# Sigmoid attention and SwiGLU on one core: an immediate bias for the scores' sigmoids, and the first gates and vals in four parts

## The chip, the core and the metric

The kernel runs on one core of a Trainium2 chip. The metric is the device time of one execution in microseconds (us). A core has a matrix engine (TensorE, "PE" in the profile; its weight loads are listed apart as "PEld"), a vector engine (DVE), a scalar engine that evaluates functions such as the sigmoid (ACT), a general one (GpSimd, "POOL"), and a sync engine that starts transfers here (SP). Each engine runs its own queue of instructions in order, and they wait for one another through semaphores. Matmuls write into PSUM, which has eight banks; each bank holds a 128 x 512 tile of 32-bit numbers.

## The reference

For 8 batches and 12 heads, 448 positions and 64 features per head:

```python
scores = q @ k.T / sqrt(64) - log(448)
attn = sigmoid(scores)                  # no softmax
x = (attn @ v), heads side by side      # 3584 x 768
g = x @ w_gate                          # 768 -> 1536
val = x @ w_val
out = (g * sigmoid(g) * val) @ w_out    # 1536 -> 768
```

The bias of the sigmoid, -log(448), is one number for the whole kernel.

## The kernel before

The attention is cut into 24 units (three for each batch, four heads each). A unit's q and k are loaded, cast to 16 bits into `src`, and transposed into `qkT`: by TensorE for the first six units (line 382), by DMA afterwards (line 408). Its scores are made in seven *bursts* (line 425) of four 64x64 matmuls each, into two banks; each burst is followed by two sigmoids on ScalarE (`sig`, line 446), which read the banks and write the tile `pt`. When enough `pt` tiles are there, the PV matmuls (line 466) multiply them with v, and two casts give two feature chunks `xT` of 128 features each. So a batch has six feature chunks, j = 0 to 5, and unit 0 gives j = 0 and 1, unit 1 gives 2 and 3, unit 2 gives 4 and 5.

The sigmoid takes its bias from a tile of one column, `sbiast`, that is filled once at the start (line 226).

The feed-forward part works through a batch in twelve tiles of 128 hidden features, two at a time (`f1`). For a pair, `joint` makes the gates (`ps_g`) and later the vals (`ps_v`): 48 matmuls each, in *quarters*, that is, in 64x64 pieces of the array (line 517). The upper 64 rows of the array write to the bank of one tile of the pair while the lower 64 rows write to the bank of the other; then the two change places. So a gate has two halves (t = 0 and 1) of 24 matmuls over all six chunks j. Between the halves stands a *turn* (line 502): a no-op on ScalarE that waits for the last matmuls of the first half and for which the first matmuls of the second half wait. ScalarE then makes the sigmoid of the gates (`s`, line 542; no bias), VectorE multiplies it with the gate (`t`, line 548) and with the vals (`hT`, line 555). The output product (`ps_o`) and its sums come later and are not touched.

Weights of gate and val come in four chunks of 384 hidden features: chunk 0 serves the tiles 0 to 2, chunk 1 the tiles 3 to 5, and so on. Each is loaded in three pieces (j in pairs) and cast by GpSimd (line 340). `ORDER` fixes the order of the loads on SP's queue: units 2 and 3 before chunk 0, unit 4 before chunk 1, unit 5 before chunk 2, unit 6 before chunk 3.

The order of the instructions on each engine is not written by hand. Every piece of work is an `op` with an engine, a planned duration, what it depends on, and the banks or buffers that it takes and gives. A dependency can have a lead: the op may begin so long before the other ends. `list_schedule` plays the program with these durations, always taking the first ready op in the order of writing within a window (40 for TensorE, 30 for ScalarE), and what comes out is the order in which the instructions are issued. The planned duration of a sigmoid of the scores is 0.445 us. Once issued, the order on an engine is fixed, and real times follow from the semaphores.

Of the kernel before, what the change touches and what calls it, by code (L numbers as in the profile page):

```python
# [13 lines left out]
SIGM = mybir.ActivationFunctionType.Sigmoid  # L14
# [41 lines left out]
STICK = 0.2  # L56
NEAR = 12
SPREAD = 3
SLOW = 1.0
LATE = 0.1  # L60
FIRST = ()
# [121 lines left out]
def kernel(  # L183
# [10 lines left out]
    nc = tc.nc  # L194

    B, H, S, D = q.shape
# [57 lines left out]
    def op(*a, **kw):  # L254
        o = Op(*a, **kw)
        ops.append(o)
        return o
# [73 lines left out]
    def load_w(w, dst, c, j2, nm):  # L331
        def fl():
            T[nm, c, j2] = staging()[:, 0:2 * CW].rearrange("p (j f) -> p j f", j=2)
            nc.sync.dma_start(
                out=T[nm, c, j2],
                in_=w[j2 * 256:(j2 + 1) * 256, c * CW:(c + 1) * CW].rearrange(
                    "(j p) f -> p j f", p=128))

        def fc():
            nc.gpsimd.tensor_copy(out=dst[c][:, 2 * j2:2 * j2 + 2, :], in_=T[nm, c, j2])  # L340
        uses[0] += 1
        ld = op("SP", 0.6, fl, take=["st"], desc=(256, CW * 4))
        R.setdefault(("w", nm, c), []).append((fc, ld))

    def load_wc(c):
        for w, dst, nm in ((moe_w_gate, wg16, "wg"), (moe_w_val, wv16, "wv")):
            for j2 in range(KC // 2):
                load_w(w, dst, c, j2, nm)

    def cast_wc(c):  # L350
        for nm in ("wg", "wv"):
# [89 lines left out]
    def sig(key, dep, slot):  # L441
        def fn(a):
            def go():
                if a == 0:
                    T[("pt",) + key] = sb.tile([128, 2, S], FP16, tag="pt", bufs=slots["pt"], name="pt")
                nc.scalar.activation(out=T[("pt",) + key][:, a], in_=T[("sc",) + key][a][:, 0:S], func=SIGM, bias=sb_t,  # L446
                                     scale=qkscale)
            return go
        x = op("ACT", 0.445, fn(0), deps=[dep], take=["pt"], give=slot[1:2])
        R["pt ring", key] = x.take  # L450
        R["sig"] = R[("pt",) + key] = op("ACT", 0.445, fn(1), deps=[x and (x, LAT["ACT"] + LATE)], give=slot[:1] + slot[2:])

    def pv(i):

# [40 lines left out]
    def after_ins(x, y):  # L495
        tc.add_manual_dep(x, y.name, mybir.DependencyInfo(mybir.DependencyClass.Sync, mybir.DependencyReason.DATA))

    def turn(a, n):

        def fn():  # L500
            e = {"DVE": nc.vector, "ACT": nc.scalar, "POOL": nc.gpsimd}[TURN]
            T["turn", n()] = e.nop().ins
            for x in T["half", n()]:
                after_ins(T["turn", n()], x)
        return op(TURN, 0.07, fn, deps=[a])

    def quarters(steps, t, n):

        for k, two in enumerate(steps):
            for row in range(2):
                o, w, x = two[row ^ t]
                rs = slice(64 * row, 64 * row + 64)
                for col in range(2):
                    cs = slice(64 * col, 64 * col + 64)
                    mm = nc.tensor.matmul(out=o[cs], lhsT=w[rs, cs], rhs=x[rs], start=t == 0 and k == 0,  # L517
                                          stop=t == 1 and k == len(steps) - 1)
                    if t == 0 and k == len(steps) - 1:
                        T.setdefault(("half", n), []).append(mm.ins)  # L520
                    if t == 1 and k == 0:
                        after_ins(mm.ins, T["turn", n])

    def f1(b, f):

        two = (f, f + 1)
        m, o = divmod(b, 2)

        def both(w, nm, t):
            def fn():  # L530
                if t == 0:
                    T["pair", nm, b, f] = T["pairs"] = T.get("pairs", 0) + 1
                    for n, x in enumerate(two):
                        T[nm, b, x] = bank("ps_" + nm, n)[:, 0:S]
                quarters([[(T[nm, b, x], w[x // FC][:, j, (x % FC) * 128:(x % FC + 1) * 128], T["xT", b, j]) for x in two]
                          for j in range(KC)], t, T["pair", nm, b, f])
            return fn

        def fs(f):
            def fn():  # L540
                t = T["s16", b, f] = sb.tile([128, S], FP16, tag="s16", bufs=slots["s16"], name="s16")
                nc.scalar.activation(out=t, in_=T["g", b, f], func=SIGM)  # L542
            return fn

        def ft(f):
            def fn():
                t = T["t1", b, f] = sb.tile([128, S], FP16, tag="t1", bufs=slots["t1"], name="t1")
                nc.vector.tensor_tensor(out=t, in0=T["g", b, f], in1=T["s16", b, f], op=MULT)  # L548
            return fn

        def fh(f):
            def fn():
                if o == 0 and f == 0:
                    T["hT", m] = sb.tile([128, NF, 2 * S], FP16, tag="hT", bufs=2, name=f"hT_{m}")
                nc.vector.scalar_tensor_tensor(  # L555
                    out=T["hT", m][:, f, o * S:(o + 1) * S], in0=T["v", b, f], scalar=HSC,
                    in1=T["t1", b, f], op0=MULT, op1=MULT)
            return fn
        xs = [(R["xT", b, j], 0.19 * j) for j in range(KC)]
        old = R["f2", m - 2] if m >= 2 and b % 2 == 0 else []  # L560

        def joint(w, nm, deps):
            a = None
            ws = [(x, 0.38 * n) for c in {x // FC for x in two} for n, x in enumerate(R["w16", "w" + nm, c])]
            for t in range(2):
                a = op("PE", 0.19 * KC, both(w, nm, t), mode=("Q", "Q"), take=[] if t else ["P", "P"],
                       deps=xs + deps + ws + [a and turn(a, lambda: T["pair", nm, b, f])])
                banks = banks if t else a.take
            return a, banks
        g, gbank = joint(wg16, "g", [])  # L570
        ts = []
        for n, x in enumerate(two):
            s = op("ACT", 0.45, fs(x), deps=[g], take=["s16"])
            s.first = 2
            ts.append(op("DVE", 0.54, ft(x), deps=[s], take=["t1"], give=s.take + gbank[n:n + 1]))

        def val():
            v, vbank = joint(wv16, "v", old + [(g, 1.0)])
            if f == NF - 2:
                v.give += [x for o, _ in xs for x in o.take]  # L580
            for n, (x, t) in enumerate(zip(two, ts)):
                R["hT", b, x] = op("DVE", 0.54, fh(x), deps=[v, t] + old, give=vbank[n:n + 1] + t.take)
        return val
# [164 lines left out]
    def f2_pair(x, y):  # L748

        two = (x, y)  # L750

        def make(final):
            for f, n in two:
                if n == 1:
                    f["start"](final)

            def fn(t):
                def go():
                    key = two[0][0]["key"] + two[0][1:]
                    if t == 0:  # L760
                        T["pair", key] = T["pairs"] = T.get("pairs", 0) + 1
                        for q, (f, n) in enumerate(two):
                            T[("p",) + f["key"] + (n,)] = bank("ps_o", q)[:, 0:HW]
                    quarters([[(T[("p",) + f["key"] + (n,)], f["spec"][n][0]()[:, x // 2, x % 2], f["spec"][n][1](x))
                              for f, n in two] for x in range(NH)], t, T["pair", key])
                return go
            a = None
            for t in range(2):
                a = op("PE", 0.1625 * NH, fn(t), mode=("Q", "Q"), take=[] if t else ["P", "P"],
                       deps=[d for f, n in two for d in f["spec"][n][2]()] + ([turn(a, lambda: T["pair", two[0][0]["key"] + two[0][1:]])] if t else [(x, LAT["PE"] + LATE) for x in [R.get("turn")] if x]))  # L770
                banks = banks if t else a.take
            R["turn"] = a
            for q, (f, n) in enumerate(two):
                f["P"][n] = a
                f["taken"][n] = banks[q:q + 1]
            for f, n in two:
                f["after"](n, final)
        return make
# [39 lines left out]
    for what in ORDER:  # L818
        if what[0] in "qv":
            loads(int(what.lstrip("qkv")), {"q": "qkv", "qk": "qk", "v": "v"}[what.rstrip("0123456789")])  # L820
        else:
            load_wc(int(what[1:]))
    casts(1)
    NPE = 6

# [138 lines left out]
```

## Time and profile before

| | |
|---|---|
| time, median of 3 | 412.19 us (412.06 to 412.19) |
| span in the profile | 410.0 us, TensorE clock 1.000 |
| TensorE busy | 401.5 us (98%) |
| ScalarE busy | 251.4 us (61%), of it 192.3 in 336 sigmoids of the scores |
| VectorE / GpSimd busy | 229.2 us (56%) / 131.3 us (32%) |
| read from HBM / written | 47.19 MB / 11.01 MB |

The page divides the span into 40 slices of 10.25 us and gives the busy share of each engine in tenths. In a group of instructions, the line names line of code, engine, operation, output<-inputs, shapes and count; behind the first bar are the total busy time and the mean of one in ns, behind the second the idle time of the engine ahead of such instructions and what ended it. Rows of stages give start and end of the stretch, its length, and for each engine the busy time with the number of instructions, then the clock, the DMA share and GB/s. Rows of the chain of waits give start, duration and what the chain went through.

### The profile page before, as it was taken

The numbers are of one execution on the slowest core, as the hardware profiler recorded it, in microseconds if no ns is written. First come the engines' busy times: TensorE is split into PE (matmuls) and PEld (weight loads), VectorE is DVE, ScalarE is ACT, GpSimd is POOL, SyncE is SP. The second block draws the span as 40 slices with busy tenths as digits, with TensorE's granted clock in tenths as the row PEclk, the third lists the DMA queues.
The fourth block names the chain that finished last, engine by engine and source line by source line (L and its number), as shares of the span: only waits on it lengthen the run. The fifth ranks groups of instructions, "written<-read, shape, count | busy, mean of one in ns | idle before, by whom it ended". The sixth has DMA issues, their size and how long they took to land.

```text
span 410.0 us, 17536 instructions
## 1 busy us (share of the span) xinstructions
PE 401.5 (98%) x7872; PEld 305.8 (75%) x7872; DVE 229.2 (56%) x420; ACT 251.4 (61%) x472; POOL 131.3 (32%) x194
## 2 busy tenths in 40 slices
PE   8989999999999999999999999999999999999995
PEld 3435666689977787666889877778999989997663
DVE  3424544457685457564555564645465655556874
ACT  5997789877878844378748567576576662111100
POOL 1888866556442312522322313422310200000000
PEclk9999999999999999999999999999999999999999
DMA  7999999999665518454864654663500302010335
GB/s 267 380 376 376 375 309 309 272 317 261 184 182 146 151 70 189 151 96 136 209 182 89 175 116 148 180 128 135 122 5 3 80 2 65 19 42 15 103 83 148
DMA packets 64794, 67.57 MB, mean 165 GB/s; under 512 B 35536, under 2 KB 60880, under 8 KB 64720
## 3 DMA queue, kind: packets, MB, share of 16 engines
q1 hardware_dynamic: 62864, 59.78, 51.6%
q0 software_dynamic: 1536, 6.29, 5.9%
q8 instruction: 61, 1.00, 1.0%
q10 hardware_dynamic: 320, 0.39, 0.3%
q14 instruction: 13, 0.11, 0.1%
HBM read 47.19 MB, written 11.01 MB: 142 GB/s over the span
## 4 chain that ended last, share of the span: by engine, by line
PE 90%; ACT 7%; issue 1%; DMA 1%; DVE 0%
PE ps_v L517 26%; PE ps_g L517 26%; PE ps_o L517 16%; PE ps_o L669 7%; PE ps_sc L425 7%; PE ps_pv L466 7%; ACT pt L446 6%; DMA st<-in_q_dram 1%; PE ps_tr L382 1%; ACT s L542 0%; PE ps_warm L810 0%; DVE st L678 0%; DVE src L267 0%
## 5 line engine op out<-in xcount | busy, mean ns | idle before, releaser
L446 ACT ACTIVATE pt<-ps_sc,sbiast 128x448 f16<-128x448 f32 x336 | 192.3, 656 | 62.2 <-PE ps_sc L425 62.1
L517 PE MATMUL ps_v<-xT,wv 64*64 64x448 f16 x2304 | 136.8, 350 | 0.0
L517 PE MATMUL ps_g<-xT,wg 64*64 64x448 f16 x2304 | 134.7, 350 | 0.0
L517 PEld LDWEIGHTS <-wv 64*64 64x64 f16 x2304 | 93.1, 107 | 21.3 <-issue 1.2
L517 PEld LDWEIGHTS <-wg 64*64 64x64 f16 x2304 | 92.5, 107 | 21.5 <-issue 0.8
L548 DVE TENSOR_TENSOR t<-ps_g,s 128x448 f16<-128x448 f32 x96 | 56.6, 620 | 67.5 <-ACT s L542 67.5
L555 DVE SCALAR_TENSOR_TENSOR hT<-ps_v,t 128x448 f16<-128x448 f32 x96 | 55.4, 619 | 46.2 <-PE ps_v L517 34.6
L542 ACT ACTIVATE s<-ps_g 128x448 f16<-128x448 f32 x96 | 48.4, 545 | 50.6 <-PE ps_g L517 44.7
L425 PE MATMUL ps_sc<-qkT 64*64 64x448 bf16 x672 | 78.5, 351 | 0.5 <-ACT pt L446 0.4
L269 POOL CAST v<-st 64x448 f16<-64x448 f32 (+1 forms) x72 | 40.6, 564 | 65.9 <-PE ps_pv L466 47.9
L269 POOL CAST src<-st 128x896 bf16<-128x896 f32 (+1 forms) x43 | 40.2, 937 | 60.8 <-DMA st<-in_q_dram 33.7
L517 PEld LDWEIGHTS <-hT 64*64 64x64 f16 x1080 | 53.2, 107 | 6.9 <-issue 0.2
L517 PE MATMUL ps_o<-wo,hT 64*64 64x384 f16 x648 | 49.6, 323 | 0.0
L466 PE MATMUL ps_pv<-pt,v 64*64 64x448 f16 x672 | 47.9, 351 | 1.6 <-ACT pt L446 0.9
L517 PE MATMUL ps_o<-st,s 64*64 64x384 f16 x480 | 46.1, 323 | 0.0
L517 PE MATMUL ps_o<-st,hT 64*64 64x384 f16 x432 | 42.2, 323 | 0.0
L425 PEld LDWEIGHTS <-qkT 64*64 64x64 bf16 x672 | 33.7, 107 | 11.2 <-issue 4.5
L678 DVE SCALAR_TENSOR_TENSOR osb<-ps_o,osb 128x384 f32<-128x384 f32 x63 | 32.9, 551 | 10.6 <-PE ps_o L517 6.3
L267 DVE CAST xT<-ps_pv 128x448 f16<-128x448 f32 x40 | 23.6, 618 | 24.7 <-PE ps_pv L466 24.4
L466 PEld LDWEIGHTS <-v 64*64 64x64 f16 x672 | 27.8, 107 | 12.3 <-issue 6.3
L688 POOL DMA_DIRECT2D out_dram<-osb x32 | 16.7, 526 | 60.1 <-DVE osb L678 60.1
L517 PEld LDWEIGHTS <-s 64*64 64x64 f16 x480 | 29.6, 107 | 4.3 <-issue 1.0
(44 smaller groups left out, 209.5 us busy)
## 6 DMA issues: line engine op xcount, KB each, us to landing
st<-in_q_dram SPq DMA_DIRECT2D x24, 448.0 KB, 5.1
st<-in_v_dram SPq DMA_DIRECT2D x24, 448.0 KB, 6.6
st<-in_k_dram SPq DMA_DIRECT2D x23, 448.0 KB, 5.6
out_dram<-osb POOLq DMA_DIRECT2D x32, 192.0 KB, 3.3
st<-in_moe_w_gate_dram SPq DMA_DIRECT2D x12, 384.0 KB, 9.0
st<-in_moe_w_val_dram SPq DMA_DIRECT2D x12, 384.0 KB, 8.8
st<-in_moe_w_out_dram SPq DMA_DIRECT2D x12, 384.0 KB, 7.7
out_dram<-st SPq DMA_DIRECT2D x16, 192.0 KB, 2.8
```

Source lines behind the costliest of these rows:

```text
L267: nc.vector.tensor_copy(out=o, in_=i)
L269: nc.gpsimd.tensor_copy(out=o, in_=i)
L425: nc.tensor.matmul(out=sc[a][64 * (g ^ a):64 * (g ^ a) + 64, 0:S].rearrange("k (s p) -> k s p", s=NS), lhsT=kT[r, s, 64 * g:64 * g + 64], ...
L446: nc.scalar.activation(out=T[("pt",) + key][:, a], in_=T[("sc",) + key][a][:, 0:S], func=SIGM, bias=sb_t, scale=qkscale)
L466: nc.tensor.matmul(out=T["pv", i, a][64 * g:64 * g + 64, :], lhsT=T["v16", i][r, a, s, :], rhs=T["pt", i, s][r, a, :], start=(s == 0), sto ...
L517: mm = nc.tensor.matmul(out=o[cs], lhsT=w[rs, cs], rhs=x[rs], start=t == 0 and k == 0, stop=t == 1 and k == len(steps) - 1)
L542: nc.scalar.activation(out=t, in_=T["g", b, f], func=SIGM)
L548: nc.vector.tensor_tensor(out=t, in0=T["g", b, f], in1=T["s16", b, f], op=MULT)
L555: nc.vector.scalar_tensor_tensor(out=T["hT", m][:, f, o * S:(o + 1) * S], in0=T["v", b, f], scalar=HSC, in1=T["t1", b, f], op0=MULT, op1=MULT)
L669: nc.tensor.matmul(out=T["p", m, k, n], lhsT=lhs()[:, x // 2, x % 2], rhs=rhs(x), start=x == 0, stop=x == NH - 1)
L678: nc.vector.scalar_tensor_tensor(out=c(*dst), in0=T["p", m, k, n], scalar=HREC, in1=c(*other), op0=MULT, op1=ADD)
L688: dma.dma_start(out=out[rows, cols].rearrange("(p s) d -> s p d", s=NS)[s], in_=T[("osb",) + t][64 * x:64 * x + 64, cols])
```

## The change

There are two edits with an effect on the program.

1. The sigmoid of the scores gets its bias as the number `sbias` in place of the tile `sb_t`, and its planned duration goes from 0.445 to 0.44 us.
2. For the first pair of the first batch, gates and vals are no longer cut into two halves over all six feature chunks but into four parts: half 0 over j = 0 to 3, half 1 over j = 0 to 3, half 1 over j = 4 and 5, half 0 over j = 4 and 5. The first two parts need only the features of units 0 and 1. Between parts of different halves stands a turn, so such a pair has two turns in place of one; between the two parts of half 1 there is none, only an order. The purpose is to let these matmuls start before unit 2 is done.

The remaining edits rename keys so that a turn belongs to a part, and give the weight loader an argument that is not used with this `ORDER`. The other pairs keep their two halves.

```diff
+SPLIT = "gv"
...
-                nc.scalar.activation(out=T[("pt",) + key][:, a], in_=T[("sc",) + key][a][:, 0:S], func=SIGM, bias=sb_t,
+                nc.scalar.activation(out=T[("pt",) + key][:, a], in_=T[("sc",) + key][a][:, 0:S], func=SIGM, bias=sbias,
                                      scale=qkscale)
             return go
-        x = op("ACT", 0.445, fn(0), deps=[dep], take=["pt"], give=slot[1:2])
+        x = op("ACT", 0.44, fn(0), deps=[dep], take=["pt"], give=slot[1:2])
...
-    def quarters(steps, t, n):
+    HALVES = [(0, 0, 1), (1, 0, 1)]
+
+    def quarters(steps, parts, p, key):
+        t = parts[p][0]
...
-                    mm = nc.tensor.matmul(out=o[cs], lhsT=w[rs, cs], rhs=x[rs], start=t == 0 and k == 0,
-                                          stop=t == 1 and k == len(steps) - 1)
-                    if t == 0 and k == len(steps) - 1:
-                        T.setdefault(("half", n), []).append(mm.ins)
-                    if t == 1 and k == 0:
-                        after_ins(mm.ins, T["turn", n])
+                    mm = nc.tensor.matmul(out=o[cs], lhsT=w[rs, cs], rhs=x[rs], start=p == 0 and k == 0,
+                                          stop=p == len(parts) - 1 and k == len(steps) - 1)
+                    if k == len(steps) - 1:
+                        T.setdefault(("end", key + (p,)), []).append(mm.ins)
+                    if p and parts[p - 1][0] != t and k == 0:
+                        after_ins(mm.ins, T["turn", key + (p - 1,)])
...
         def joint(w, nm, deps):
             a = None
+            parts = [(0, 0, KC), (1, 0, KC)]
+            if (b, f) == (0, 0) and nm in SPLIT:
+                parts = [(0, 0, 4), (1, 0, 4), (1, 4, KC), (0, 4, KC)]
             ws = [(x, 0.38 * n) for c in {x // FC for x in two} for n, x in enumerate(R["w16", "w" + nm, c])]
-            for t in range(2):
-                a = op("PE", 0.19 * KC, both(w, nm, t), mode=("Q", "Q"), take=[] if t else ["P", "P"],
-                       deps=xs + deps + ws + [a and turn(a, lambda: T["pair", nm, b, f])])
-                banks = banks if t else a.take
+            for p, (t, j0, j1) in enumerate(parts):
+                same = p and parts[p - 1][0] == t
+                a = op("PE", 0.19 * (j1 - j0), both(w, nm, parts, p), mode=("Q", "Q"), take=[] if p else ["P", "P"],
+                       deps=[(x, 0.19 * n) for n, (x, _) in enumerate(xs[j0:j1])] + deps + ws +
+                       [a and ((a, LAT["PE"] + LATE) if same else turn(a, (nm, b, f, p - 1)))])
+                banks = banks if p else a.take
             return a, banks
```

## The prediction

> **What bounds the kernel now.** I read the page first, then the chain of waits of the first 80 us, the weight loads counted in short stretches, the busy time by stage, and last GpSimd's timeline for the arrival of the weights.
>
> The page: TensorE is busy almost throughout, and the sigmoids of the scores are ScalarE's largest group.
>
> ```profile
> PE 401.5 (98%) x7872; PEld 305.8 (75%) x7872; DVE 229.2 (56%) x420; ACT 251.4 (61%) x472; POOL 131.3 (32%) x194
> ...
> GB/s 267 380 376 376 375 309 309 272 317 261 184 182 146 151 70 189 151 96 136 209 182 89 175 116 148 180 128 135 122 5 3 80 2 65 19 42 15 103 83 148
> ...
> L446 ACT ACTIVATE pt<-ps_sc,sbiast 128x448 f16<-128x448 f32 x336 | 192.3, 656 | 62.2 <-PE ps_sc L425 62.1
> ...
> L542 ACT ACTIVATE s<-ps_g 128x448 f16<-128x448 f32 x96 | 48.4, 545 | 50.6 <-PE ps_g L517 44.7
> ```
>
> 98% is not a dense TensorE. Weight loads per 5 us (one per matmul) show where it is dense: 108 is full. Between 20 and 30 us it runs half empty, and three later stretches have holes.
>
> ```profile
> 20.00:25.00 5.00, 1.97 (x55) 1.00 1.07 375
> 25.00:30.00 5.00, 1.73 (x48) 1.00 1.06 377
> ...
> 35.00:40.00 5.00, 3.07 (x108) 1.00 1.06 377
> ...
> 60.00:65.00 5.00, 2.94 (x89) 1.00 1.29 324
> ...
> 110.00:115.00 5.00, 3.36 (x88) 1.00 0.36 114
> ```
>
> The chain of waits says who holds it: ScalarE's sigmoids, without a gap, until 28.8 us; then the last PV and the first gate half, and from there TensorE.
>
> ```profile
> 27.91 0.85 ACT pt L446
> 28.76 0.04 issue
> 28.80 0.38 PE ps_pv L466 x3
> 29.18 0.19 PE ps_sc L425 x4
> 29.37 1.28 PE ps_g L517 x24
> ```
>
> By stage: from 6.6 to 29 us ScalarE is busy for 22.39 of 22.40 us; afterwards it has slack (34.60 of 42.00).
>
> ```profile
> 6.60:29.00 22.40, 20.54 (x231) 9.28 (x231) 8.92 (x15) 22.39 (x44) 15.43 (x22) 1.00 1.05 379
> 29.00:71.00 42.00, 41.80 (x836) 26.18 (x832) 19.52 (x34) 34.60 (x66) 31.08 (x42) 1.00 1.09 342
> ```
>
> The second resource is DMA: about 376 GB/s without a break from 10 to 50 us, so weights come when their turn comes. GpSimd's timeline (start, duration) gives the casts of chunks 1 and 3:
>
> ```profile
> 31.27 2.36 POOL L340 CAST wg<-st 128x768 f16<-128x768 f32 x3
> ...
> 35.72 0.83 POOL L340 CAST wv<-st 128x768 f16<-128x768 f32 x1 [0.23 <-DMA st<-in_moe_w_val_dram]
> ...
> 51.54 2.36 POOL L340 CAST wg<-st 128x768 f16<-128x768 f32 x3
> ```
>
> So: a stage bound by ScalarE to 28.8 us, then TensorE to the end, with DMA close behind up to about 55 us.
>
> **What the Trainium skill says.** "ScalarE: Activation LUTs", section "What ACT_TABLE_LOAD costs": with immediate scale and bias an ACTIVATE takes 186 ns + 0.833 ns per column, a [128,1] pointer operand adds about 93, and neighbours overlap by about 93. For 448 columns that is 559 and 652 ns; the trace has 545 (no bias given) and 656 (bias from a tile), so it agrees, and the pointer is the difference. "Perfetto Trace Analysis", "Identifying the Most-Contended Engine": matmul busy share misleads, weight loads are the better sign; the counts above show that here. "TensorEngine Tiling (Array Packing)", "Gotcha 1: PSUM Pressure": different row tiles may not write one bank at the same time, and software must order them; that is why a change of half needs a turn. The trace shows such turns as 17 ns semaphore events of ScalarE; no run here shows what happens without them.
>
> **The change, part by part.**
>
> *Immediate bias.* Eighteen sigmoids from 6.62 us take 9.55 us in the chain, 0.53 each; two neighbouring sigmoids of the gates take 0.98 with 0.545 for the last, so 0.435 each. I take 0.44, or 0.09 less. Up to 28.8 us there are 42 sigmoids (three units, seven bursts of two): 42 x 0.09 = 3.8 us. The inputs keep up: unit 2 is transposed and copied by 17.97 us, its first sigmoid would be due at 6.6 + 28 x 0.44 = 18.9. The end of ScalarE's stage moves from 28.8 to about 25.0. The other 294 sigmoids lie beside matmuls, except in the three holes (about 19, 20 and 12 + 4 missing weight loads at 46 ns: 0.9 + 0.9 + 0.7 = 2.5 us), where the chain reads pt, s, pt, s: ScalarE alternates and a PV waits for the last one. A step of 0.44 instead of 0.53 closes about 60% of that: 1.5 us; bounds 0 and 2.5.
>
> *Planned duration 0.445 to 0.44.* This moves no time itself. It was 0.09 too small before and fits now, so the order written by the planner and the order in which data are ready agree better. The order will still change in places; I put nothing on it, and +/-1 us in the range.
>
> *First gates in four parts.* Steps 0 to 3 use features of units 0 and 1 (copied by 23.0 us) and gate chunk 0 (cast by 23.7). Two parts of four steps are 2 x 16 x 47.5 ns = 1.5 us that can fill the half-empty stretch before 25 us. The rest, 0.76 us, still waits for unit 2. Added: one turn, on ScalarE's queue. Behind this no-op stand sigmoids, for which PV and the next bursts wait; if the matmuls of the part are late, ScalarE stands still. The event is 17 ns; the wait I bound by 0 and by the 0.35 us that a weight load waited for the only such turn in this stage; I take 0.15. The two gate banks are also held some 3 us longer.
>
> *First vals in four parts.* They start only once the gates are in their last part, when all features are there: nothing is moved ahead, and one more turn is added, with other matmuls beside it. Cost 0 to 0.35, I take 0.15.
>
> *Names, keys, the argument of the weight loader:* same instructions, no time.
>
> *What DMA leaves of it.* 3.8 + 1.5 = 5.3 us would bring the second gate pair from 35.82 us to 30.5. But gate chunk 1 is cast only by 33.63, and its last third is needed 0.76 us after the start: not before 32.9, a shift of 2.9. Meanwhile TensorE may run ahead with scores and PV of unit 3: ScalarE can do about 13 sigmoids from 25.0 to 32.9 where before 8 were done by 35.8, so 2.5 bursts more (0.5 us), and with four slots ready the first PV part (0.76 us). Shift at this point: 2.9 to 4.1. The same for chunk 3: cast by 53.9, pair (8,9) started at 55.88, at best 53.1, and 5 bursts and one PV (2.3 us) can be ahead: 2.8 to 5.1. I take 3.8. The split then adds little to what the bias alone brings, since its 1.5 us run mostly into the wait for chunk 1.
>
> Sum: 3.8 (start, after DMA) + 1.5 (holes) - 0.3 (turns) = 5.0 us; 412.2 - 5.0 = 407.2.
>
> **Rivals.**
>
> *DMA takes more (0.15).* TensorE has nothing to run ahead with, because the score banks or the planner's order don't give it: 2.8 us at chunks 1 and 3, holes not closed, turns 0.3: 2.5 us gained, 409.7. For it: DMA at 376 GB/s. Against: ScalarE's slack after 29 us.
>
> *All of it arrives (0.22).* The run ahead covers the whole wait: 5.3 less turns 0.3, plus 2.2 in the holes: 7.2 gained, 405.0. For it: bound 5.1 at chunk 3. Against: bound 4.1 at chunk 1.
>
> *Not faster (0.10).* Scores starve: eight banks serve two bursts (4), a PV (2), the gates (2). With the gates held early and a transpose asking for a bank, only one burst is in flight; then each sigmoid pair also waits for matmul and semaphore, about 0.5 us. Over the nine bursts from 23 us on this is 4.5 us, which cancels the gain of the bias, and the turns and later holes add 0.5 to 1: 412.7. For it: exactly eight banks. Against: before, scores run with PV and transposes in the same stage and ScalarE never waits.
>
> **How the numbers follow.** The likeliest case has 0.53 and gives 407.2. The range 404.7 to 410.0 takes in the DMA case, most of the full case and +/-1 us of order; left out are the not-faster case and the far end of the full one. Faster by over 0.2% (below 411.4): 0.53 + 0.15 + 0.22 and a little less, 0.89; within 0.2%: 0.04; slower: 0.07, both from the last rival.
>
> **What would show it.** Sigmoid group at 545 to 565 ns instead of 656; ScalarE's unbroken stage ending near 25 us; gate matmuls before the last PV of unit 2; gate chunk 1 cast again near 33.6 us, now with TensorE thin just before; the weight loads of the later holes closer to 108. I am wrong if the sigmoids stay at 656, if ScalarE shows waits for scores between 20 and 26 us, or if the gain at 56 us is gone by the end.

## The result, and the profile after

The changed kernel takes 407.07 us (median of four, 406.61 to 409.60), the kernel before beside it 412.13 (412.06 to 412.19): 5.1 us less, ratio 0.9891 with a 95% interval of 0.9856 to 0.9926. On a second chip the ratio was 0.9865 (0.9829 to 0.9900). The new kernel's times are spread more widely than the old one's in the first comparison, and the profile on record is of its slowest execution, 409.60 us. So its span of 407.6 us shows less of the gain than the median.

The page of the changed kernel, as before: engines, then the two groups of sigmoids (mean of one in ns behind the busy time).

```profile
PE 400.1 (98%) x7871; PEld 306.8 (75%) x7873; DVE 230.0 (56%) x420; ACT 223.2 (55%) x472; POOL 132.7 (33%) x194
...
L448 ACT ACTIVATE pt<-ps_sc 128x448 f16<-128x448 f32 x336 | 162.7, 550 | 77.8 <-PE ps_sc L427 77.3
...
L546 ACT ACTIVATE s<-ps_g 128x448 f16<-128x448 f32 x96 | 48.1, 545 | 59.0 <-PE ps_g L522 50.0
```

The sigmoids of the scores went from 656 to 550 ns, close to the 545 of the gates' sigmoids, which never had a bias tile; `sbiast` is gone from their inputs. TensorE's busy time hardly moved: the gain can't be read there.

Weight loads in stretches of 5 us, changed kernel (the number behind x is the count; 108 is dense):

```profile
20.00:25.00 5.00, 2.16 (x61) 1.00 1.07 376
25.00:30.00 5.00, 2.52 (x83) 1.00 1.06 376
55.00:60.00 5.00, 2.75 (x93) 1.00 1.10 237
60.00:65.00 5.00, 3.50 (x100) 1.00 1.36 367
110.00:115.00 5.00, 4.29 (x103) 1.00 0.36 109
```

From 20 to 30 us there are 144 where there were 103, and the hole at 110 us shrank: 103 instead of 88. The hole at 60 us has 100 instead of 89, but a new, thinner stretch is ahead of it: from 55 to 65 us together there are 193 where there were 197. In this profile that hole moved rather than shrank.

The chain of waits at the end of ScalarE's stage, changed kernel:

```profile
25.23 1.51 ACT pt L448 x4
26.74 0.10 issue
26.84 0.02 ACTq L504
26.85 0.07 issue
26.92 1.09 ACT pt L448 x2
28.01 0.04 issue
28.06 0.38 PE ps_pv L468 x3
28.43 0.76 PE ps_g L522 x16
```

L504 is the turn. TensorE's timeline has the gates beside it:

```profile
25.00 1.38 PE L522 MATMUL ps_g<-xT,wg 64*64 64x448 f16 x16
...
28.07 1.13 PE L522 MATMUL ps_g<-xT,wg 64*64 64x448 f16 x16
```

Only the first part, 16 matmuls or 0.76 us, runs ahead of the last PV of unit 2. The second part needs no features of unit 2 either, and its turn is done at 26.86 us, but in the planned order it stands behind that PV. It is so in every profile with four parts: the split moves half of the 1.5 us ahead that the prediction counted.

ScalarE's stage ends at 28.01 us, not near 25. The beginning of the chain says why. Before (first fence) and changed kernel (second):

```profile
4.97 0.85 PE ps_tr L382 x10
5.82 0.43 PE ps_warm L810 x2
6.25 0.37 PE ps_sc L425 x4
6.62 2.72 ACT pt L446 x5
```

```profile
5.05 1.25 PE ps_tr L384 x10
6.30 0.85 PE ps_warm L818 x2
7.16 0.89 PE ps_sc L427 x8
8.04 0.97 PE ps_warm L818 x2
```

Here two filling matmuls took 0.85 us in place of 0.43: in this execution TensorE ran at half speed until about 9.5 us. In the program the transposes, scores and fillers of the start are the same in kind; the first sigmoid came 1.1 us later, all but 0.1 of it by this, and afterwards ScalarE, now quicker, waited for scores (idle ahead of it 1.22, 0.53, 0.26 us at 7.7, 10.1 and 12.4 us).

### The profile page after: what moved, and what is told of

Same layout as the page of the kernel before. It is cut to its first block, busy times and chain, and to the rows that moved or that the text cites. A ratio compares the mean times of both kernels' runs of the same rounds, so it can differ in the third digit from the quotient of the medians.

```text
span 407.6 us, 17541 instructions
## 1 busy us (share of the span) xinstructions
PE 400.1 (98%) x7871; PEld 306.8 (75%) x7873; DVE 230.0 (56%) x420; ACT 223.2 (55%) x472; POOL 132.7 (33%) x194
## 4 chain that ended last, share of the span: by engine, by line
PE 95%; ACT 2%; DMA 1%; issue 1%; DVE 0%; ACTq 0%
PE ps_v L522 27%; PE ps_g L522 27%; PE ps_o L522 16%; PE ps_sc L427 8%; PE ps_pv L468 7%; PE ps_o L678 7%; ACT pt L448 2%; PE ps_warm L818 1%; PE ps_tr L384 1%; DMA st<-in_q_dram 1%; DVE st L687 0%; DVE src L268 0%; ACTq L504 0%
## 5 line engine op out<-in xcount | busy, mean ns | idle before, releaser
L448 ACT ACTIVATE pt<-ps_sc 128x448 f16<-128x448 f32 x336 | 162.7, 550 | 77.8 <-PE ps_sc L427 77.3
L522 PEld LDWEIGHTS <-wg 64*64 64x64 f16 x2304 | 93.7, 107 | 22.2 <-issue 2.4
L427 PE MATMUL ps_sc<-qkT 64*64 64x448 bf16 x672 | 77.2, 354 | 0.1
L270 POOL CAST v<-st 64x448 f16<-64x448 f32 (+1 forms) x72 | 41.5, 577 | 60.0 <-PE ps_pv L468 42.5
L522 PEld LDWEIGHTS <-hT 64*64 64x64 f16 x1080 | 52.2, 107 | 7.0 <-issue 0.2
L468 PE MATMUL ps_pv<-pt,v 64*64 64x448 f16 x672 | 45.3, 350 | 0.1
L522 PE MATMUL ps_o<-st,hT 64*64 64x384 f16 x432 | 41.2, 323 | 0.0
L687 DVE SCALAR_TENSOR_TENSOR osb<-ps_o,osb 128x384 f32<-128x384 f32 x63 | 32.9, 550 | 10.4 <-PE ps_o L522 6.6
L468 PEld LDWEIGHTS <-v 64*64 64x64 f16 x672 | 26.6, 107 | 9.1 <-issue 2.7
```

Source lines behind the costliest of these rows:

```text
L270: nc.gpsimd.tensor_copy(out=o, in_=i)
L427: nc.tensor.matmul(out=sc[a][64 * (g ^ a):64 * (g ^ a) + 64, 0:S].rearrange("k (s p) -> k s p", s=NS), lhsT=kT[r, s, 64 * g:64 * g + 64], ...
L468: nc.tensor.matmul(out=T["pv", i, a][64 * g:64 * g + 64, :], lhsT=T["v16", i][r, a, s, :], rhs=T["pt", i, s][r, a, :], start=(s == 0), sto ...
L687: nc.vector.scalar_tensor_tensor(out=c(*dst), in0=T["p", m, k, n], scalar=HREC, in1=c(*other), op0=MULT, op1=ADD)
```

## The experiments

All kernels were timed beside the kernel before, runs 1 to 4, 5 to 8 and 9 to 12 on one chip each. The ratios are to the kernel before on the same chip, with 95% intervals.

**1. The changed kernel again.** No edit.

> The changed kernel once more, for a second profile and five more times. In the first profile the first ten transposes took 1.25 us where before they took 0.85, and two filling matmuls 0.85 in place of 0.43, so TensorE ran at about half speed from 5 to 9 us. Theory A (a start that is slow in some executions and quick in others, with the queue of TensorE behind it): single times spread over 2 to 3 us, 406.5 to 409.6, and a profile with a quick start shows the first sigmoid at 6.6 us instead of 7.7 and ScalarE without gaps from there to about 25 us. Rival B (the 409.6 is an outlier of another cause): the start is slow in this profile too, at a time near 407.

Ratio 0.9865 (0.9829 to 0.9900), times 406.80 to 410.41. In this profile the ten transposes took 1.04 us and the first sigmoid began at 6.85; ScalarE's 42nd sigmoid ended at 26.39 instead of 28.01. Still the span is 407.1, only 0.5 less. The chain shows what took the place of the start (changed kernel, second profile):

```profile
50.52 0.57 POOL v L270
...
51.15 0.46 POOL v L270
...
51.75 0.57 POOL v L270
...
52.37 2.38 POOL wg L341 x3
54.75 0.04 issue
54.79 0.56 PE ps_g L522 x6
```

TensorE now waits for the cast of gate chunk 3, which itself came behind the cast of unit 6's v. In this stretch the weight loads fall to 70:

```profile
45.00:50.00 5.00, 3.12 (x108) 1.00 1.06 376
50.00:55.00 5.00, 1.83 (x70) 1.00 1.38 305
55.00:60.00 5.00, 3.19 (x108) 1.00 0.87 248
```

So the spread is real, but Theory A holds only in part. This execution began 0.9 us earlier than the one on record and was, at 409.11 us, only 0.5 us quicker. At the gates of the tiles 8 and 9, the first that need chunk 3, the two are level (table below); by the end of batch 0 run 1 leads by 1.2 us, and by the first output product by 0.5 again. A part of the spread thus arises after the start.

**2. The bias alone; 3. the four parts alone.**

Run 2, against the changed kernel:

```diff
-SPLIT = "gv"
+SPLIT = ""
```

Run 3:

```diff
-                nc.scalar.activation(out=T[("pt",) + key][:, a], in_=T[("sc",) + key][a][:, 0:S], func=SIGM, bias=sbias,
+                nc.scalar.activation(out=T[("pt",) + key][:, a], in_=T[("sc",) + key][a][:, 0:S], func=SIGM, bias=sb_t,
```

> Immediate bias and planned duration as in the change, gates and vals in two halves as before. Theory A (the bias carries it, the split's head start runs mostly into the wait for weight chunk 1): 407.3 us, within 0.6 of the changed kernel, and the second gate pair starts near 33 us. Rival B (the two parts add up: 1.5 us of matmuls moved ahead are 1.5 us at the end): about 408.6. Rival C (the split carries it): 410 or more.

> Four parts and the planned 0.44 us, but the bias again from the tile. Theory A: ScalarE's stage still ends near 28.8 us, two gate parts (1.5 us) move ahead of it, less 0.3 for turns: about 410.9. Rival (the turn on ScalarE's queue or the banks held longer cost more than the head start): 412 to 413. Rival C (the split carries the change): 408 or less.

Bias alone: 0.9882 (0.9854 to 0.9910), 408.62 us. Four parts alone: 0.9931 (0.9906 to 0.9956), 410.75 us. Both together, same chip: 0.9865. The bias brings most, and the four parts alone don't make the change; but they brought 0.7%, twice what I had worked out (1.2 us, 0.3%), with the longer sigmoids still in one unbroken row of 44 from 6.79 us. The size is uncertain: on this chip the kernel before itself took 412.41 to 415.64 us, and between the profiles on record (spans 410.0 and 409.0) the difference is 1.0 us, near what I had worked out. The intervals of the bias alone and of the full change overlap too much to say what the parts add on top; run 10 serves that.

**4. Eight filling matmuls instead of six, changed kernel.**

```diff
-NWARM = 6
+NWARM = 8
```

> The changed kernel with eight filling matmuls at the start instead of six, so that TensorE is busy from 1.2 us up to the first transposes near 5 us without the pause of 0.7. If the slow starts come from that pause: no time over 407.3, median 406.6, transposes in 0.85 us. If they come by chance of the clock's phase alone: the same spread as the changed kernel. If the two matmuls push the transposes back: 0.2 to 0.4 slower.

0.9848 (0.9819 to 0.9877), 406.72 to 408.23 us: neither the limit of 407.3 nor the old spread (406.80 to 410.41 in run 1). The profile has a quick start, and it is the clearest view of the change undisturbed. ScalarE's timeline (start, duration, idle time ahead in brackets):

```profile
6.64 3.60 ACT L448 ACTIVATE pt<-ps_sc 128x448 f16<-128x448 f32 x8 [0.54 <-PE ps_sc L427]
10.43 4.71 ACT L448 ACTIVATE pt<-ps_sc 128x448 f16<-128x448 f32 x10 [0.19 <-PE ps_sc L427]
15.30 11.61 ACT L448 ACTIVATE pt<-ps_sc 128x448 f16<-128x448 f32 x26 [0.16 <-PE ps_sc L427]
```

26 sigmoids in 11.61 us, with the gates' two banks taken from 23.0 us on, and no gap: the banks do not starve the scores, and the first turn, which ScalarE carries out at 24.9 us, costs it nothing. The last 14 of the first 42 come at 0.436 us each, the first 28 at 0.474: at the start the scores hold the quicker ScalarE back by 1.1 us in all. The chain of this kernel up to 54 us goes through loads and casts only, and ends thus:

```profile
40.32 9.01 DMA st<-in_v_dram
...
51.30 2.38 POOL wg L341 x3
53.68 0.04 issue
53.73 0.57 PE ps_g L522 x6
```

**5. The planned 0.44 us alone; 6. the bias with the planned 0.445.**

Run 5 has the edits of runs 2 and 3 together, which leaves the planned duration. Run 6 has the edit of run 2 and, for both sigmoids of a burst:

```diff
-        x = op("ACT", 0.44, fn(0), deps=[dep], take=["pt"], give=slot[1:2])
+        x = op("ACT", 0.445, fn(0), deps=[dep], take=["pt"], give=slot[1:2])
```

> The kernel before with the planned duration 0.44 us alone: bias from the tile, two halves. Theory A (the planned number moves no time of its own): within 0.3% of before. Rival D (part of what the four parts brought alone, 0.7% where 0.3% was worked out, is a luckier order from the new planned number): 0.3 to 0.5% faster than before.

> Immediate bias alone, the planned 0.445 us and two halves kept. Theory A: 1.1 to 1.2% faster than before, like the run with both. Rival D: 0.7 to 0.9% faster, the rest being the planned number's.

0.44 alone: 1.0011 (0.9990 to 1.0033), nothing. Bias with 0.445: 0.9902 (0.9879 to 0.9924), 409.11 us; within the interval of run 2. The planned number has no part in the gain that can be measured, so Rival D falls, and the 0.7% of run 3 belong to the parts themselves.

**7. Four parts for the gates only.**

```diff
-SPLIT = "gv"
+SPLIT = "g"
```

> The changed kernel with the gates in four parts and the vals in two halves. Theory A (the vals' parts move nothing ahead and add a turn): the same as the changed kernel within 0.1%, or up to 0.15 us faster. Rival (the vals' first part starts earlier because it waits for fewer features): 0.1 to 0.3% slower than the changed kernel.

0.9887 (0.9862 to 0.9911), 408.73 us, on another chip than run 1 (0.9865). The intervals overlap; a difference of 0.2% either way can't be told. What the vals' parts cost or bring stays open. This profile had a slow start (transposes 1.25 us).

**8. The v of units 4 to 6 behind the weights.**

```diff
-ORDER = "v1 q2 q3 w0 q4 w1 q5 w2 q6 w3".split()
+ORDER = "v1 q2 q3 w0 qk4 w1 v4 qk5 w2 v5 qk6 w3 v6".split()
```

> The changed kernel with the v of units 4, 5 and 6 loaded after the weight chunk that followed it, so that the weights of chunks 1, 2 and 3 arrive one 448 KB load (1.2 us) earlier; nothing else is moved. Theory A (the first 55 us are held by the arrival of the weights, and the gate matmuls of the pair (8,9) wait for gate chunk 3): 0.8 to 1.2 us (0.2 to 0.3%) faster than the changed kernel, gate chunk 3 cast 1.2 us earlier, and the TensorE wait for it shorter by about as much. Rival E (the wait is made up later by TensorE, or another one takes its place at once, such as the transposes of unit 5 and 6): the same time within 0.1%.

0.9875 (0.9846 to 0.9905), 406.53 to 410.41 us. Gate chunk 3 is cast by 52.63 us and the wait is gone; weight loads of this kernel:

```profile
45.00:50.00 5.00, 3.06 (x108) 1.00 1.06 374
50.00:55.00 5.00, 3.12 (x108) 1.00 1.25 326
55.00:60.00 5.00, 2.89 (x99) 1.00 1.03 301
```

But the time is the same as that of the full change on the other chips. Theory A's step "wait removed, time gained" fell: the plan put the vals of the second pair ahead of the gates of the third (these start at 40.64 us instead of 35.96 in run 1), and the first half of the gates (8,9) ends at 54.32, no earlier than the 54.29 of run 4 with the wait. The loss stands earlier: both kernels start their second gate pair at 33.0 to 33.1 us, but by then this one has done 84 PV matmuls, not 100, and 104 of the scores, not 108. Those 20 matmuls are still to come, some 0.95 us at 47.5 ns, and the wait in run 4 was 1.2 us (that half takes 2.31 us there instead of 1.14).

**9 to 12. Four kernels with eight filling matmuls, beside one another:** the kernel before, the bias alone, the full change, and the full change with the v of run 8.

> The kernel before with eight filling matmuls at the start instead of six. Its single times on the later chips lay between 412.1 and 415.6 us. If the spread comes from starts at half speed and the filling matmuls prevent them: 412.0 to 412.8, so up to 0.3% under the kernel before on the same chip. If not: the same spread.

> Immediate bias and planned 0.44 us, two halves, eight filling matmuls. Theory A (the bias carries nearly all, because the head start of the four parts runs into the wait for the weight chunks 1 and 3): 407.3 to 407.9 us, within 0.15% of the run with four parts. Rival B (the parts add up): 0.3 to 0.4% slower than the run with four parts, 408.3 to 408.8.

> The changed kernel with eight filling matmuls again, beside the other three: 406.7 to 408.2 us as in its first run, and 1.2 to 1.3% under the kernel before with eight.

> The same with the v of units 4 to 6 after the weight chunks. Theory A (the wait for chunk 3 is real time at the end): gate chunk 3 cast by 52.6 us, no wait of the pair (8,9), 0.1 to 0.25% faster than the run with eight filling matmuls alone. Rival E (made up later): the same within 0.05%.

| eight fillers | ratio to before (six) | times, us |
|---|---|---|
| before | 0.9988 (0.9978 to 0.9999) | 412.02 to 413.81 |
| bias alone | 0.9895 (0.9875 to 0.9914) | 407.79 to 409.63 |
| full change | 0.9856 (0.9836 to 0.9875) | 406.82 to 407.64 |
| full change, v late | 0.9863 (0.9842 to 0.9883) | 406.41 to 408.49 |

Three things follow. Eight fillers are worth 0.1% to the kernel before and lessen the spread (its times with six were 412.04 to 415.41); they do not abolish slow starts, as two of these four profiles still have the transposes at 1.27 us. The full change is 0.39% better than the bias alone, with no time in common: Rival B, the parts add up. But these are four and five executions, and the two intervals touch at 0.9875; with six fillers the same pair, runs 1 and 2, differed by 0.17%, within the scatter. And the late v brings nothing here either that can be measured: Rival E.

Landmarks read from the traces, in us, with two profiles of the full change with eight fillers (runs 4 and 11); (8,9) is the pair of the tiles 8 and 9:

| | before | changed, on record | run 1 | runs 4, 11 | bias alone (10) |
|---|---|---|---|---|---|
| first sigmoid | 6.61 | 7.72 | 6.85 | 6.64, 6.60 | 7.49 |
| 42nd sigmoid ends | 28.75 | 28.01 | 26.39 | 26.03, 27.03 | 26.88 |
| first gate matmul | 29.02 | 25.00 | 23.38 | 23.02, 24.02 | 27.15 |
| second gate pair starts | 35.82 | 35.12 | 33.50 | 33.14, 34.14 | 33.80 |
| gate chunk 3 cast | 53.90 | 53.53 | 54.74 | 53.67, 54.36 | 54.10 |
| gates (8,9), first half ends | 57.19 | 55.26 | 55.36 | 54.29, 54.98 | 55.09 |
| last vals of batch 0 end | 70.20 | 68.51 | 67.31 | 66.25, 66.94 | 68.50 |
| first output product | 141.85 | 139.96 | 139.49 | 137.17, 137.86 | 140.03 |
| end | 409.98 | 407.55 | 407.06 | 404.72, 405.47 | 407.61 |

The profiles of runs 10 and 11 show where these two executions part. At the gates (8,9) both are level, 55.09 and 54.98, because the full change has waited for chunk 3. A difference of 1.56 us opens between there and the end of batch 0, and another 0.6 by the first output product. Weight loads of the bias alone (first) and of the full change (second):

```profile
50.00:55.00 5.00, 3.12 (x108) 1.00 1.27 323
55.00:60.00 5.00, 2.69 (x88) 1.00 1.08 206
```

```profile
50.00:55.00 5.00, 2.64 (x94) 1.00 1.32 325
55.00:60.00 5.00, 3.20 (x108) 1.00 0.95 276
```

The one without the split has its hole 5 us later. Its chain there goes through a gate's sigmoid:

```profile
56.60 1.16 PE ps_g L522 x24
57.76 0.02 issue
57.78 0.55 ACT s L546
58.34 0.20 issue
58.53 0.38 PE ps_sc L427 x4
```

20 missing loads at 46 ns are 0.9 us of the 1.56. That the split is the cause is not shown. Run 10 began slowly (first sigmoid at 7.49 us) and run 11 quickly (6.60), and no profile of the bias alone began quickly (7.08 to 7.83). From the first half of the gates (8,9) to the end of batch 0 run 10 takes 13.41 us and runs 1, 4 and 11 take 11.95 to 11.96; but the changed kernel's profile on record, with four parts and a slow start, takes 13.25 and has its thin stretch at the same place (93 loads from 55 us). Run 2, the bias alone with six fillers, takes 12.80 and has 102 loads there. So the hole may hang on the moment at which a kernel arrives, and not on the split alone.

## Why the prediction was right, and where it was not

**The sum held: 407.2 forecast, 407.07 measured. That it held so closely is in part luck: its two large terms were off, the first too big and the second too small.** The landmarks let them be checked in the two profiles of the full change with eight fillers, runs 4 and 11.

- *Start, after DMA: 3.8 us.* This was the shift at the pair (8,9): at least 2.8 us by the arrival of chunk 3, the rest work that TensorE would have ahead, up to five bursts and one PV. The first half of these gates ends earlier by 57.19 - 54.29 = 2.9 us in run 4 and by 57.19 - 54.98 = 2.2 in run 11. When the pair starts, TensorE is one burst ahead (152 score matmuls instead of 148, 0.19 us) and no PV (140 in both). So the term came to 3.1 and 2.4 us. Here the rival "DMA takes more" was nearer.
- *Holes: 1.5 us.* From there to the end the shift grows to 5.3 and 4.5, that is by 2.4 and 2.3; without the burst 2.2 and 2.1. The weight loads agree: in 10 us around the hole at 60 (57 to 67 us) and 15 us around each of those at 110 and 130 (105 to 120, 125 to 140) 63 are missing before, 24 in run 4 and 18 in run 11. At 46 ns these are 1.8 and 2.1 us. So size and sign fit, and the term was somewhat too small; the share of 60% for which it stands had no working behind it.
- *Turns: 0.3 us.* Not resolved; the run that would show half of it lies within the scatter. The first turn cost ScalarE nothing (run 4).

**Right in its steps:** the price of the pointer operand (93 ns a sigmoid by the Trainium skill, "ScalarE: Activation LUTs", section "What ACT_TABLE_LOAD costs"; 106 measured between 656 and 550, and 91 from start to start, 527 and 436; the 559 and 652 ns in the prediction are estimates from that page's formula), the start of the gates between 23 and 25 us, though of one part and not two, the gates (8,9) held until chunk 3 (in runs 1 and 4 their first half stands waiting for exactly that cast and ends at 55.36 and 54.29, where a start at 53.1 gives 54.2), and the banks, which starved nothing. The second gate pair came not before 32.9 us (33.14 and 33.50 in these runs), but not for the reason given: TensorE had work up to there and shows no wait for a cast of chunk 1.

**Wrong: the end of ScalarE's stage.** I took 42 x 0.09 = 3.8 us and an end at 25.0 us. The step itself came out at 0.436 us as worked out, but in run 4, with a quick start, the 42 sigmoids take 26.03 - 6.64 = 19.4 us, 0.46 each, because of the waits for scores. So the end moves by 2.7 us, in run 11, which waits another 1.0 us for scores at 11.2 us, by 1.7, and in the profile on record by 0.7. I had checked that the inputs of unit 2 are there in time, and not that the fixed queue of TensorE, with its fillers and transposes, keeps delivering scores at the quicker step. Whether the kernel before hides a slow start behind its longer sigmoids is not shown: its profiles have the first sigmoid at 6.55 to 6.82 us.

**Wrong: the share of the four parts.** I wrote that the split "adds little to what the bias alone brings, since its 1.5 us run mostly into the wait for chunk 1". It brings 0.7% alone (run 3, as uncertain in size as said there) and 0.39%, 1.6 us, on top of the bias (runs 10 and 11). The wait that does bind is that for chunk 3, and it levels runs 10 and 11 at 55 us; what sets them apart behind it is open, as said above.

**What stays open.** Removing the wait for chunk 3 gained nothing in two runs. That wait is then not by itself the loss that my bound made of it: in another order of the same work an equal loss stood earlier, and which of the edits to the order costs what was not separated.

## What to carry to other kernels

A bias that is one number belongs in the instruction: as a column tile it cost 0.09 us in each step of an unbroken row of sigmoids here, and where they were the bound it set the time. When a bounding engine is made quicker, look for the next bounds; here they were a load's arrival and the neighbour's queue, a microsecond or two behind. Work out both before counting the whole saving. And where the order is planned, the value of an edit is known only together with the others: compare the edits alone and together, on one chip.

## What the runs showed of the hardware that was not expected

How long TensorE stays at half speed differs from execution to execution, even of the same program. In all 14 profiles the fillers begin at 1.19 us and come 0.43 us apart; later they come about 0.22 us apart. What differs is when they change over. The traces also hold the moment from which the full clock was granted, and it agrees with that change: 4.28 us in the profile before, 9.48 in the changed kernel's on record, 5.68 in run 1 (the same program), 10.36 in run 2. With it go the ten transposes (0.83 to 1.27 us), two filling matmuls behind them (0.43 to 0.85) and the first sigmoid (6.55 to 8.17, the latest after a later first load as well). The clock column reads 1.00 in all these stretches, as that view counts no loss before this first record. The Trainium skill, "TensorE: Matmul & The Clock Gate", section 'Part 1: The HAM clock gate (the "warmup" mystery)', says that the clock is released after some 3.4 us of activity measured in windows that run free of the kernel, so that the number of slow matmuls varies by run. The two speeds and the varying moment agree with that; that the phase of such a window is the cause was not tried. Filling most of the pause ahead of the first transposes narrowed the spread of the kernel before from 3.4 to 1.8 us, over 27 and 22 executions.
